# Batch 2 by transposed loads, early output tiles as 64x64 products, and a new order

## The chip, the cores and the metric

The kernel runs on one core of one Trainium2 chip. The metric is the device time of one execution in microseconds. The core has TensorE (PE; its weight loads are the row PEld), VectorE (DVE), ScalarE (ACT), GpSimd (POOL) and SyncE (SP), and 16 DMA engines, which all queues share. SP and POOL issue the DMAs of this kernel (ScalarE two at the start); each has a queue of its own.

## The reference

```python
# q, k, v: (8, 12, 448, 64); w_in (768, 2048), w_out (2048, 768)
scores = matmul(q, k.T) / sqrt(64)
m = max(scores)
e = exp(scores - m)
attn = e / (sum(e) + exp(-m) + 1e-09)
x = matmul(attn, v)            # heads side by side: (3584, 768)
h = x @ w_in
out = square(maximum(h, 0)) @ w_out
```

Attention for 8 batches of 12 heads, 448 tokens and head size 64, and then a two-layer block with a squared ReLU over all 3584 tokens.

## The kernel before

Everything is computed in fp16 with fp32 sums. A "quad" is four heads of a batch (three quads a batch). Scores are computed keys by queries, without the maximum: `e = exp(score)`, and the sum of `e` comes from an addition on VectorE and a product with ones. So a quad takes seven score steps (64 keys each), seven `exp` steps on ScalarE, four additions on VectorE, seven steps of values, and a reciprocal by Ln and Exp on ScalarE.

Scores need q and k with the 64 head dimensions on the partitions. There are two ways to get them.

- Batches in `ON_PE` (0, 1 and 2): POOL loads them in natural layout with a cast to fp16 (`load_natural_quads`, line 112), TensorE transposes them (`transpose_one`, line 194, 14 products for one of q or k of a quad), and VectorE or ScalarE copies them from PSUM into the tile `qk` (`transposed_copy`, line 201). A score step is then four 64x64 products of 448 columns.
- The others: POOL writes an fp16 copy of q and k of the batch to DRAM (`stage`, line 143), SP loads it transposed in three DMAs (`transposed_loads`, line 160: q, and k twice, shifted by a row), POOL copies the last keys apart (`tail_keys`, line 171), and V comes in four DMAs with another order of tokens. A score step is then eight 64x64 products of 224 columns.

The tile `qk` has two buffers, so batch 2's takes that of batch 0.

The whole is emitted in an order written out by hand (`ORDER`, line 662), whose steps are one letter with numbers (`STEPS`, line 624). It covers batch 0 (in halves of 224 queries), batches 1 and 2, and the first six output tiles. Its steps:

- `d` a load from the list `LOADS` (line 614), `c t u` the first quad's casts, transposes and copies, `T U` `transpose_one` and `transposed_copy` of (batch, quad, q or k)
- `s e` scores and exp. 0 to 23 are the halves of batch 0, 24 to 44 batch 1, 45 to 65 batch 2, seven steps a quad
- `p b y z n x` values, additions, sum, Ln, reciprocal and normalization of batch 0; `v a S Z M X` the same of a quad of the batches 1 and 2
- `i r g` a pair of first-layer blocks of batch 0, its ReLU and its square; `j k l` the same of one block of 128 of F of batch 1
- `o n,f0,f1` blocks f0 to f1 of the 16 blocks of F of output tile n (128 tokens by 384 columns; n even is the left half, n odd the right half), `O` its evacuation and store
- `P` closes the first PSUM pools and opens the ring of four banks, from which the tiles `mp` come

Each engine takes its instructions in this order, and so do the DMA queues of SP and POOL.

From batch 3 on five cycles follow (`CYCLE`, line 719), one a batch: the last quad of the batch before, scores and values of this one, output tiles `o`, `O`, `Q` and the first layer `j k l` of the batch before. Their output tiles are already computed as 64x64 products in two half sums (`out_piece` with `rows`, line 536): each block is four products, the upper 64 rows of F into one bank and the lower 64 into another. `O` (`out_first`) scales the first sum, `Q` (`out_second`) adds the other one, and only then is the tile stored. The six early tiles are single 128x128 products in one bank, with `out_done` (line 566).

In `store` (line 522) the tokens of a batch in `ON_PE` go out in pieces of 64 rows, of the others in pieces of up to 128.

Of the kernel before, what the change touches and what calls it, by code (L numbers as in the profile page):

```python
# [10 lines left out]
FP16 = mybir.dt.float16  # L11
# [5 lines left out]
def kernel(  # L17
# [9 lines left out]
    nc = tc.nc  # L27

    B, H, S, D = q.shape
# [4 lines left out]
    RUN = 4  # L34
    NQ = H // 4
    KC = S // 64
    ON_PE = (0, 1, 2)
    COLS = H * S // 2 + 16
    HALF = DM // 2
    FIRST = S // 2  # L40
# [55 lines left out]
    def load_v_quads(b, g0=0, g1=NQ):  # L96
        if b not in vns:
            vns[b] = v_pool.tile([128, 2, NQ, KC, D], FP16, name="vn")
        vn = vns[b]
        if b in ON_PE:  # L100
            if g1 - g0 == NQ:
                nc.gpsimd.dma_start(out=vn.rearrange("p j g c d -> p (j g) (c d)"), in_=by_pairs["v"][b])
            else:
                nc.gpsimd.dma_start(out=vn[:, :, g0].rearrange("p j c d -> p j (c d)"), in_=by_pairs["v"][b, :, g0::NQ])
            return
        for i in range(2):
            rows_ = vn[64 * i:64 * i + 64].rearrange("p j g c d -> p (j g) (c d)")
            for c0, c1 in ((0, KC - 1), (KC - 1, KC)):
                src = v[:, :, 64 * c0:64 * c1].rearrange("b (hp i) (p t) d -> b i p hp (t d)", i=2, t=c1 - c0)
                nc.gpsimd.dma_start(out=rows_[:, :, c0 * D:c1 * D], in_=src[b, i])  # L110
# [32 lines left out]
    def stage(b):  # L143
        for n, t in (("q", q), ("k", k)):
# [11 lines left out]
            if hi < lo + TOTAL:  # L156
                nc.gpsimd.dma_start(out=st[hi - lo:TOTAL].rearrange("(r w) -> r w", r=1),
                                    in_=src[0:lo + TOTAL - hi].rearrange("(r w) -> r w", r=1))

    def transposed_loads(b):  # L160
        qk = qks[b] = qk_pool.tile([128, 3, COLS], FP16, name="qk")
        for i, n, x, c in ((0, "q", FRONT, H * S // 2), (1, "k", FRONT, H * S // 2), (2, "k", 0, COLS)):
            nc.sync.dma_start(
                out=qk[:, i, 0:c],
                in_=stages[n, b][x:x + c * 2 * D].rearrange("(r c) -> r c", c=2 * D),
                transpose=True,
            )

    kms = {}

    def tail_keys(b):

        km = kms[b] = flat.tile([128, H, 64], FP16, name="flatq")
        for r in range(2):
            for odd in range(2):
                rows_ = slice(64 * r, 64 * r + 64)
                which, x = (1, 0) if odd == r else (2, odd)
                src = qks[b][rows_, which, x:x + H * S // 2].rearrange("p (h x) -> p h x", h=H)
                nc.gpsimd.tensor_copy(km[rows_].rearrange("p h (x o) -> p h x o", o=2)[:, :, :, odd],  # L179
                                      src[:, :, S // 2 - 32:S // 2])  # L180
# [418 lines left out]

    def load_quad(b, g):  # L600

        x = {(0, 1): (0, 0), (0, 2): (0, 1), (1, 0): (1, 0), (1, 1): (0, 0), (1, 2): (0, 1),
             (2, 0): (1, 0), (2, 1): (1, 1), (2, 2): (0, 0)}[b, g]
        if (b, x[0]) not in nats:
            nats[b, x[0]] = nat.tile([128, RUN * 2 * S], FP16, name=f"nn{x[0]}")
        load_natural_quads(b, (g,), x[1], nats[b, x[0]])

    def load_third():
# [2 lines left out]
        load_v_quads(3)  # L611
        stage(4)

    LOADS = ([lambda b=b, g=g: load_quad(b, g) for b in range(3) for g in range(NQ) if b + g]
             + [lambda b=b, g=g: load_v_quads(b, g, g + 1) for b in range(2) for g in range(NQ)]
             + [lambda: load_v_quads(2)]
             + [lambda i=i: load_win(i, NW) for i in range(NW)]
             + [lambda n0=n0, y=y: load_wout(n0, y, 2) for n0 in (0, HALF) for y in range(2)]
# [2 lines left out]
    def quad_visit(n):  # L621
# [29 lines left out]
        "v": lambda m, c: values_step(m, c),  # L651
        "X": lambda m: quad_x(m),
        "P": lambda n: other_ring(),
        "o": lambda n, f0, f1: out_piece(128 * (n // 2), HALF * (n % 2), HALF, range(f0, f1)),
        "O": lambda n, act: out_done(128 * (n // 2), HALF * (n % 2), HALF, act),
    }

    def other_ring():
# [1 line left out]
        ring.append(ctx.enter_context(tc.tile_pool(name="ring", bufs=4, space=bass.MemoryType.PSUM)))  # L660

    ORDER = """
        d0 W8 c1,4,0 c0,0,1 c1,0,1 t0,0,0 c0,4,1 t1,0,0 u0,0,0,0 t1,0,4 u1,0,0,0 t0,0,4 u1,0,4,0 s0 d8 d1 u0,0,4,0 t0,1,0 e0 t1,1,0 u0,1,0,0 u1,1,0,0 s1 s2 e1
        d10 t0,1,4 u0,1,4,0 t1,1,4 u1,1,4,1 T0,1,0 T0,1,1 s3 U0,1,0,0,4,0 e2 U0,1,1,0,4,0 s4 U0,1,0,4,7,1 e3 d9 U0,1,1,4,7,0 d2 p0 e4 p2 s16 p1 e16 b0,0 b0,1
        p3 b0,2 b0,3 s6 y0 d18 s5 T0,2,0 e6 U0,2,0,0,4,0 z0 T0,2,1 U0,2,1,0,4,0 e5 U0,2,1,4,7,0 U0,2,0,4,7,0 s7 s9 b1,0 n0 b1,1 e7 x0 s8 p4 e9 b1,2 d3 b1,3 p5
        e8 p6 p7 s10 y1 b2,0 p8 p9 e10 s11 p10 b2,1 z1 e11 b2,2 b2,3 s12 p11 s13 n1 x1 y2 e12 T1,0,0 U1,0,0,0,7,0 T1,0,1 z2 n2 s14 e13 x2 p12 p13 s15
        U1,0,1,0,7,0 e14 e15 s17 p14 b3,0 b3,1 e17 s18 i0,7 d17 d5 b3,2 e18 b3,3 p15 y3 z3 b4,0 r0,7,0 s21 s19 e21 T1,1,1 d4 n3 b4,1 i0,6 U1,1,1,0,7,0 s20 d15
        T1,1,0 x3 b4,2 e19 b4,3 d16 s23 p16 p17 p18 r0,6,0 U1,1,0,0,7,0 e20 b5,0 e23 s22 e22 b5,1 p19 y4 s26 z4 n4 i0,4 g0,7 x4 r0,4,0 s27 i0,5 g0,6 b5,2 e26
        s25 e27 T1,2,1 s28 e25 p20 p21 r0,5,0 p22 s24 g0,5 b5,3 e28 d11 T1,2,0 p23 e24 s29 y5 e29 U1,2,1,0,7,0 U1,2,0,0,7,0 T2,0,0 T2,0,1 U2,0,0,0,7,0 z5 g0,4
        d6 U2,0,1,0,7,0 s30 n5 s32 a0,0 e30 d13 i0,0 i0,1 s33 x5 e32 r0,0,0 g0,0 r0,1,0 s31 i1,0 d12 g0,1 e33 i0,3 r1,0,0 e31 r0,3,1 s35 d7 s36 e35 P0 e36  # L670
        i0,2 s34 e34 a0,1 a0,2 g1,0 v0,0 a0,3 S0 v0,1 v0,2 v0,3 v0,4 Z0 v0,5 v0,6 M0 r0,2,0 g0,3 g0,2 s37 i1,3 a1,0 a1,1 e37 X0 r1,3,0 a1,2 g1,3 i1,6 s39 s40
        a1,3 e39 i1,1 r1,1,0 r1,6,0 s43 T2,2,0 e40 d20 T2,2,1 g1,6 e43 s42 g1,1 e42 U2,2,0,0,7,0 s41 d19 i1,5 r1,5,0 e41 s38 e38 T2,1,0 T2,1,1 U2,2,1,0,7,0
        U2,1,0,0,7,1 S1 a2,0 Z1 s44 U2,1,1,0,7,0 i1,4 i1,2 a2,1 e44 r1,4,1 s45 a2,2 g1,5 a2,3 v1,0 v1,1 M1 v1,2 v1,3 v1,4 v1,5 v1,6 r1,2,1 v2,0 S2 v2,1 X1
        g1,4 e45 g1,2 v2,2 v2,3 v2,4 Z2 v2,5 v2,6 M2 s47 X2 s46 i1,7 j3,0,2 r1,7,0 o0,0,4 j3,2,4 j1,0,2 j3,4,6 k3,0 j12,0,2 o0,4,8 j1,2,4 o0,8,12 e46 e47
        o0,12,16 s50 d21 g1,7 s51 j12,2,4 j1,4,6 k1,0 j5,0,2 e51 e50 l3 j5,2,4 j5,4,6 d23 O0,1 k5,1 j12,4,6 l5 o1,0,4 s48 s49 j6,0,2 e49 l1 e48 d22 k12,1 l12
        o1,4,8 o1,8,12 o1,12,16 s53 s52 e52 e53 j6,2,4 j10,0,2 o5,0,4 j6,4,6 O1,1 s55 k6,0 s54 j10,2,4 o5,4,8 j0,0,2 e55 a3,0 j10,4,6 j8,0,2 o5,8,12 j0,2,4
        a3,1 k10,1 o5,12,16 e54 s61 s57 l6 a4,0 j14,0,2 O5,0 e57 j14,2,4 j14,4,6 e61 j8,2,4 a3,2 j9,0,2 j9,2,4 j0,4,6 j9,4,6 a3,3 j8,4,6 l10 s56 k0,0 k14,0
        e56 l0 k8,1 s58 o2,0,4 o2,4,8 l14 d14 s59 v4,0 v4,1 v4,2 v4,3 a4,1 v4,4 v4,5 e58 k9,0 s60 e59 s64 o2,8,12 d24 l9 o2,12,16 a4,2 a4,3 j7,0,2 e60 v4,6
        e64 S4 Z4 M4 O2,0 S3 j7,2,4 o4,0,4 l8 o4,4,8 o4,8,12 o4,12,16 j7,4,6 Z3 s62 X4 s63 M3 O4,0 v3,0 v3,1 v3,2 v3,3 v3,4 v3,5 e62 v3,6 s65 X3 k7,1 j4,0,2
        e65 o3,0,4 a5,0 o3,4,8 o3,8,12 o3,12,16 j15,0,2 j4,2,4 j4,4,6 l7 e63 j15,2,4 a5,1 j2,0,2 O3,1 a5,2 j2,2,4 a5,3 j15,4,6 k4,0 j13,0,2 j11,0,2 S5 Z5  # L680
        k15,0 M5 l4 l15 j2,4,6 k2,0 j13,2,4 l2 j11,2,4 j13,4,6 j11,4,6 k11,1 k13,1 l11 l13
    """

    for step in ORDER.split():
# [4 lines left out]
    def cycle(b):  # L689
        m = NQ * (b - 1) - 1  # L690
        first = EARLY + KC * (b - 3)

        def following():
            if b + 1 < B:
                transposed_loads(b + 1)
                tail_keys(b + 1)
                load_v_quads(b + 1)
                if b + 2 < B:
                    stage(b + 2)

        return {
# [20 lines left out]
        a1,1 o2,8,10 o2,10,12 o2,12,14 s2,3 o2,14,16 o3,0,2 s2,2 O2,0 o3,2,4 a1,2 Q2 o3,4,6 e2,3 e2,2 o3,6,8 s2,6 e2,6 o3,8,10 s2,0 e2,0 o3,10,12  # L722
        o3,12,14 o3,14,16 a1,3 s2,4 o5,0,2 e2,4 o5,2,4 o5,4,6 o5,6,8 s2,5 O3,0 s2,1 o5,8,10 o5,10,12 o5,12,14 o5,14,16 e2,5 e2,1 Q3 S1 v1,0 v1,1 Z1
        v1,2 v1,3 M1 v1,4 O5,0 v1,5 Q5 v1,6 X1 o6,0,2 s3,4 e3,4 o6,2,4 s3,0 e3,0 o6,4,6 o6,6,8 a2,0 o6,8,10 o6,10,12 s3,1 o4,0,2 o6,12,14 a2,1 s3,3
        e3,1 o4,2,4 o6,14,16 s3,2 e3,3 o4,4,6 O6,1 a2,2 o4,6,8 s3,5 a2,3 o4,8,10 Q6 o4,10,12 e3,2 e3,5 o4,12,14 o4,14,16 O4,1 Q4 a3,0 s3,6 v2,0 v2,1
        S2 Z2 v2,2 v2,3 v2,4 v2,5 M2 v2,6 e3,6 X2 j2,0,2 j2,2,4 j2,4,6 k2,0 j13,0,2 j13,2,4 l2 j13,4,6 j3,0,2 k13,1 l13 j3,2,4 j15,0,2 j12,0,2 j15,2,4
        j0,0,2 j3,4,6 a3,1 j15,4,6 k3,1 a3,2 k15,1 j12,2,4 a3,3 l15 j0,2,4 j0,4,6 l3 j12,4,6 j10,0,2 j10,2,4 j4,0,2 k0,0 l0 k12,1 l12 j10,4,6 j6,0,2
        j7,0,2 j7,2,4 j7,4,6 j4,2,4 k10,0 j6,2,4 j4,4,6 l10 j6,4,6 k7,1 j5,0,2 l7 j5,2,4 k4,1 j11,0,2 k6,0 j11,2,4 j11,4,6 j9,0,2 l6 j5,4,6 l4 j9,2,4
        j8,0,2 j8,2,4 k5,1 j9,4,6 l5 j1,0,2 k11,0 j8,4,6 j1,2,4 j1,4,6 k9,1 j14,0,2 j14,2,4 l11 l9 k8,0 j14,4,6 l8 k1,1 l1 k14,0 S3 Z3 d0 l14 M3
    """  # L730

    for b in range(3, B):
# [58 lines left out]
```

## Time and profile before

| | us |
|---|---|
| median of 3 runs (lowest, highest) | 396.51 (396.07, 397.43) |
| the profiled execution | 396.87 |
| its span, first to last instruction | 394.8 |
| one cycle (178.11 to 223.45, and on to 268.62, 313.79) | 45.2 to 45.3 |
| end of ORDER, start of the cycles | 105.9 |

The profiled execution's own time is 2.1 us over its span, and 0.1% over the median. TensorE's granted clock is 1.00 in all windows. Busy times are unions of what an engine's instructions cover; a matmul's own duration (0.32 us for 384 columns) has the length of the pipeline in it, so the price of a matmul is read from start to start.

Some groups of the page, in the form: line, engine, operation, tiles written and read, shapes, count, busy us and mean ns.

| group | count | mean ns |
|---|---|---|
| L208 DVE COPY, a transposed quad into `qk`, 128x896 | 11 | 619 |
| L206 ACT the same | 1 | 911 |
| L563 DVE the add of `Q`, 128x384 | 35 | 556 |
| L559 DVE the scaling of `O`, 128x384 | 23 | 556 |
| L557 ACT the scaling of `O`, 128x384 | 32 | 491 |
| L245 ACT exp of a score step, 128x896 | 122 | 917 |
| L179 POOL COPY, a part of `tail_keys` | 20 | 643 |

DMAs: a natural quad is two of 224 KB, a quad's V 224 KB, a piece of `win` 384 KB (eight of them), a piece of `wout` 768 KB (four), a staged q or k 676 KB. All of these KB count what is written.

### The profile page before, as it was taken

To read this page: it belongs to the slowest core of one execution; us is meant where nothing else is said; L and a number is where in the kernel's file an instruction comes from. 1 tells how busy PE (TensorE), PEld (TensorE's weight loads), DVE (VectorE), ACT (ScalarE), POOL (GpSimd) and SP (SyncE) were. 2 spreads that over 40 slices of the span, in tenths; PEclk is the share of its full clock that TensorE was granted. 3 is DMA by queue.
4 is the path that set the end of the run, shared out by engine and by line. 5 is a ranking of instruction groups with operands and counts; after the bars stand their busy time and mean duration, and the time that the engine had idled before them with its cause. 6 is when DMAs were issued, how large, how long until landed. Compare 5 with 4: busy or idle time off the path is not lost.

```text
span 394.8 us, 13877 instructions
## 1 busy us (share of the span) xinstructions
PE 385.5 (98%) x6252; PEld 262.9 (67%) x6252; DVE 240.5 (61%) x445; ACT 238.1 (60%) x324; POOL 59.8 (15%) x96
## 2 busy tenths in 40 slices
PE   8789999999999999999999999999999999999997
PEld 4567776445599766896579866776677765555665
DVE  3889994385746765668536876567646785285000
ACT  4999895768479625895279834896269934100111
POOL 8354500003200032000500016000500000000000
PEclk9999999999999999999999999999999999999999
DMA  8999999568942579419692398527652100100222
GB/s 146 203 204 206 203 206 208 98 127 154 191 85 63 113 140 181 96 43 161 113 203 75 77 193 127 129 64 141 126 74 68 58 7 2 62 0 14 68 80 81
DMA packets 75051, 45.33 MB, mean 115 GB/s; under 512 B 47472, under 2 KB 72944, under 8 KB 74992
## 3 DMA queue, kind: packets, MB, share of 16 engines
q0 software_dynamic: 24752, 22.62, 36.3%
q1 hardware_dynamic: 49952, 21.59, 25.0%
q8 instruction: 49, 0.80, 0.8%
q10 hardware_dynamic: 288, 0.23, 0.2%
q14 instruction: 10, 0.08, 0.1%
HBM read 45.69 MB, written 17.93 MB: 161 GB/s over the span
## 4 chain that ended last, share of the span: by engine, by line
PE 94%; DVE 3%; ACT 1%; issue 1%; DVEq 0%; ACTq 0%
PE mp L92 81%; PE sp L92 9%; PE xp L92 2%; PE mp L198 2%; ACT et L245 1%; DVE qk L208 1%; DVE half L334 1%; DVE half L332 0%; PE mp L225 0%; ACT rcp L356 0%; ACT rcp L363 0%; DVE qk L235 0%; DVE half L338 0%; DVE half L336 0%; DVE rt L496 0%
## 5 line engine op out<-in xcount | busy, mean ns | idle before, releaser
L92 PE MATMUL mp<-wout,gs 64*64 64x384 f16 (+2 forms) x2592 | 166.7, 322 | 0.0
L92 PE MATMUL mp<-xt,win 128*64 128x448 f16 (+2 forms) x1344 | 151.4, 339 | 0.1
L245 ACT ACTIVATE et<-sp 128x896 f16<-128x896 f32 (+1 forms) x131 | 110.8, 889 | 30.1 <-PE sp L92 28.9
L92 PEld LDWEIGHTS <-win 128*64 128x64 f16 (+1 forms) x1344 | 89.6, 106 | 58.7 <-issue 7.4
L92 PEld LDWEIGHTS <-gs 64*64 64x64 f16 (+1 forms) x2592 | 105.9, 106 | 34.3 <-issue 1.1
L494 ACT ACTIVATE rt<-mp 128x448 f16<-128x448 f32 x55 | 29.3, 544 | 57.2 <-PE mp L92 52.4
L500 DVE TENSOR_TENSOR gs<-rt 128x448 f16<-128x448 f16 x128 | 49.2, 401 | 22.2 <-ACT rt L494 19.8
L92 PE MATMUL sp<-qk 64*64 64x224 f16 (+1 forms) x1056 | 57.4, 274 | 2.5 <-issue 0.9
L496 DVE TENSOR_SCALAR rt<-mp 128x448 f16<-128x448 f32 x73 | 45.2, 621 | 23.0 <-PE mp L92 21.5
L557 ACT ACTIVATE ot<-mp 128x384 f32<-128x384 f32 (+2 forms) x34 | 16.4, 481 | 51.3 <-PE mp L92 50.8
L92 PEld LDWEIGHTS <-qk 64*64 64x64 f16 x1056 | 36.1, 114 | 14.4 <-issue 7.4
L179 POOL COPY flatq<-qk 64x384 f16<-64x384 f16 x20 | 12.4, 643 | 205.9 <-DMA qk<-stage_k 205.6
L245 ACT ACTIVATE nn<-sp 128x896 f16<-128x896 f32 x42 | 36.7, 915 | 1.9 <-PE sp L92 1.8
L478 DVE TENSOR_TENSOR xt<-mp,rcp 128x448 f16<-128x448 f32 x42 | 24.3, 620 | 20.0 <-ACT rcp L457 17.8
L92 PEld LDWEIGHTS <-vn 64*64 64x64 f16 x756 | 24.1, 107 | 9.8 <-issue 2.6
L563 DVE SCALAR_TENSOR_TENSOR ot<-mp,ot 128x384 f32<-128x384 f32 x35 | 19.5, 556 | 16.9 <-ACT ot L557 15.3
L454 ACT ACTIVATE rcp<-sp,one_b 128x896 f32<-128x896 f32 x21 | 21.2, 1007 | 10.0 <-PE sp L92 10.0
L92 PE MATMUL mp<-et,vn 64*64 64x448 f16 (+1 forms) x448 | 25.1, 343 | 0.0
L559 DVE TENSOR_SCALAR ot<-mp 128x384 f32<-128x384 f32 x23 | 12.8, 556 | 19.6 <-PE mp L92 19.5
L432 DVE TENSOR_TENSOR half<-et 128x1792 f16<-128x1792 f16 x15 | 16.3, 1087 | 7.0 <-ACT et L245 6.9
L457 ACT ACTIVATE rcp<-rcp 128x896 f32<-128x896 f32 x21 | 20.0, 952 | 0.6
L434 DVE TENSOR_TENSOR half<-half,et 128x1792 f16<-128x1792 f16 x15 | 16.4, 1091 | 0.7 <-ACT et L245 0.3
(59 smaller groups left out, 198.2 us busy)
## 6 DMA issues: line engine op xcount, KB each, us to landing
out_dram<-ot SPq DMA_DIRECT2D x52, 96.0 KB, 2.3
out_dram<-ot SPq DMA_DIRECT2D x19, 192.0 KB, 1.9
win<-in_moe_w_in_dram POOLq DMA_DIRECT2D x8, 384.0 KB, 11.1
wout<-in_moe_w_out_dram POOLq DMA_DIRECT2D x4, 768.0 KB, 15.6
vn<-in_v_dram POOLq DMA_DIRECT2D x10, 288.0 KB, 4.8
stage_q<-in_q_dram POOLq DMA_DIRECT2D x4, 676.0 KB, 8.8
stage_k<-in_k_dram POOLq DMA_DIRECT2D x4, 676.0 KB, 12.0
nn<-in_q_dram POOLq DMA_DIRECT2D x8, 224.0 KB, 8.1
```

Of the source, the lines that this page charges most:

```text
L92: return nc.tensor.matmul(out_, lhsT, rhs, start=start, stop=stop)
L245: nc.scalar.activation(out=out_, in_=in_, func=AF.Exp, scale=scale)
L432: nc.vector.tensor_add(esq[m], a[:, 0:w], a[:, w:2 * w])
L434: nc.vector.tensor_add(esq[m], esq[m], z[:, 0:w])
L454: nc.scalar.activation(out=rcp, in_=zp[:, :, 0:S], func=AF.Ln, bias=one_b)
L457: nc.scalar.activation(out=zqs[m], in_=zqs[m], func=AF.Exp, scale=-1.0)
L478: nc.vector.tensor_mul(xts[b][:, 2 * g + i, :], xqs[m][i][:, 0:S], zqs[m][:, i, :])
L494: nc.scalar.activation(out=rt[:, 0:m], in_=hp[:, 0:m], func=AF.Relu)
L496: nc.vector.tensor_scalar(out=rt[:, 0:m], in0=hp[:, 0:m], scalar1=0.0, scalar2=None, op0=ALU.max)
L500: nc.vector.tensor_mul(gs[:, f0:f0 + per, t0 % RING:t0 % RING + n], r, r)
L557: nc.scalar.activation(out=ot, in_=op[:, 0:w], func=AF.Copy, scale=OUT_SCALE)
L563: nc.vector.scalar_tensor_tensor(out=ot, in0=lo[:, 0:w], scalar=OUT_SCALE, in1=ot, op0=ALU.mult, op1=ALU.add)
```

## The change

1. `ON_PE` loses batch 2: its q and k are staged, loaded transposed, and its tail keys copied; `T2`, `U2` steps and three natural quads go. Its V comes in the four DMAs of the later batches, its scores are eight products of 224 columns, and its stores are in pieces of up to 128 rows.
2. The early tiles' `o` steps use `rows`, and `O` and `Q` replace `out_done`.
3. ORDER is another one. The loads of POOL now run `d0 d1 d8 d2 d10 d9 d3 d18 d15 d17 d16 d4 d5 d11 d19 d20 d12 d21 d13 d22 d7 d23 d14`, then `d24`, where `d5` is `stage(2)`, `d7` `tail_keys(2)`; `d6` is `transposed_loads(2)`, on SP. (Before: `d0 d8 d1 d10 d9 d2 d18 d3 d17 d5 d4 d15 d16 d11 d6 d13 d12 d7 d20 d19 d21 d23 d22 d14 d24`, where `d5`, `d6`, `d7` were natural quads of batch 2.)
4. In the cycles the one step `d0` becomes seven, with k loaded before q, and they stand before `a3,0` and no longer at the end.

```diff
-    ON_PE = (0, 1, 2)
+    ON_PE = (0, 1)
...
+    PLANES = (("k", FRONT, H * S // 2), ("k", 0, COLS), ("q", FRONT, H * S // 2))
+
+    def transposed_load(b, i):
+        qk = qk_of(b)
+        n, x, c = PLANES[i]
+        nc.sync.dma_start(
+            out=qk[:, (i + 1) % 3, 0:c],
+            in_=stages[n, b][x:x + c * 2 * D].rearrange("(r c) -> r c", c=2 * D),
+            transpose=True,
+        )
+
     def transposed_loads(b):
-        qk = qks[b] = qk_pool.tile([128, 3, COLS], FP16, name="qk")
-        for i, n, x, c in ((0, "q", FRONT, H * S // 2), (1, "k", FRONT, H * S // 2), (2, "k", 0, COLS)):
...
+        for i in range(3):
+            transposed_load(b, i)
...
-    LOADS = ([lambda b=b, g=g: load_quad(b, g) for b in range(3) for g in range(NQ) if b + g]
-             + [lambda b=b, g=g: load_v_quads(b, g, g + 1) for b in range(2) for g in range(NQ)]
+    LOADS = ([lambda b=b, g=g: load_quad(b, g) for b in ON_PE for g in range(NQ) if b + g]
+             + [lambda: stage(2), lambda: transposed_loads(2), lambda: tail_keys(2)]
+             + [lambda b=b, g=g: load_v_quads(b, g, g + 1) for b in ON_PE for g in range(NQ)]
...
-        "o": lambda n, f0, f1: out_piece(128 * (n // 2), HALF * (n % 2), HALF, range(f0, f1)),
-        "O": lambda n, act: out_done(128 * (n // 2), HALF * (n % 2), HALF, act),
+        "o": lambda n, f0, f1: out_piece(128 * (n // 2), HALF * (n % 2), HALF, range(f0, f1), True),
+        "O": lambda n, act: out_first(128 * (n // 2), HALF * (n % 2), HALF, act),
+        "Q": lambda n: out_second(128 * (n // 2), HALF * (n % 2), HALF),
...
+        c0,0,1 d0 c1,4,0 W8 c1,0,1 t0,0,0 u0,0,0,0 t1,0,0 c0,4,1 u1,0,0,0 t1,0,4 t0,0,4 u0,0,4,1 s0 d1 d8 u1,0,4,0 t0,1,0 u0,1,0,0 t1,1,0 s1 d2
...
+        g0,6 b5,0 p19 y4 b5,1 z4 n4 i0,0 i0,1 g0,7 s26 e27 x4 b5,2 p20 r0,0,0 r0,1,1 b5,3 s25 e26 e25 p21 p22 p23 y5 i0,5 g0,0 r0,5,0 s29 s24 z5 g0,1
+        n5 x5 g0,5 i0,4 i1,1 r0,4,0 e24 e29 r1,1,1 s28 d19 e28 s30 e30 P0 a0,0 i0,3 i1,4 a0,1 g1,1 g0,4 s33 s31 r1,4,0 r0,3,0 a0,2 g1,4 e33 i1,6
+        T1,2,0 T1,2,1 e31 U1,2,1,0,7,0 r1,6,0 s32 s34 d20 e32 i1,0 U1,2,0,0,7,1 g0,3 i0,2 e34 i1,5 s37 s35 g1,6 d12 r1,0,0 e37 i1,7 e35 r0,2,0 a0,3 S0
+        v0,0 v0,1 Z0 s40 v0,2 g1,0 r1,7,0 v0,3 v0,4 v0,5 v0,6 M0 s39 g0,2 e40 r1,5,0 a1,0 d21 d13 i1,2 s41 X0 e39 o0,0,4 e41 o0,4,8 s36 g1,7 r1,2,1
+        g1,2 s38 i1,3 e36 g1,5 s43 e38 o0,8,12 o0,12,16 e43 O0,1 a1,1 r1,3,0 s42 s44 g1,3 d22 o4,0,4 o4,4,8 e42 o4,8,12 a2,0 d6 a1,2 a1,3 Q0 s56
+        o4,12,16 e44 O4,1 S1 a2,1 Q4 a2,2 v1,0 v1,1 v1,2 a2,3 d7 v1,3 v1,4 Z1 e56 o2,0,4 o2,4,8 v1,5 S2 v1,6 M1 o2,8,12 o2,12,16 d23 X1 Z2 v2,0 v2,1
+        v2,2 v2,3 O2,1 Q2 v2,4 s53 o5,0,4 s45 v2,5 v2,6 M2 e53 s49 o5,4,8 e45 s60 X2 e49 o5,8,12 o5,12,16 s54 e60 s55 j8,0,2 O5,0 e54 j7,0,2 j7,2,4 Q5
...
-        def following():
+        def following(n):
             if b + 1 < B:
-                transposed_loads(b + 1)
-                tail_keys(b + 1)
-                load_v_quads(b + 1)
-                if b + 2 < B:
+                if n < 3:
+                    transposed_load(b + 1, n)
+                elif n < 5:
+                    tail_keys(b + 1, (n - 2,))
+                elif n == 5:
+                    load_v_quads(b + 1)
+                elif b + 2 < B:
                     stage(b + 2)
...
-        ... k1,1 l1 k14,0 S3 Z3 d0 l14 M3
+        ... O4,1 Q4 d0 d3 d6 d1 d4 d2 d5 a3,0 s3,6 ...
+        ... k1,1 l1 k14,0 S3 Z3 l14 M3
```

`tail_keys(b, planes)` copies, for each plane of k given, the two halves of partitions that come from it, instead of all four copies at once.

## The prediction

> **What bounds the kernel now.** I read the page's busy times first, then the chain that ended last.
>
> ```profile
> PE 385.5 (98%) x6252; PEld 262.9 (67%) x6252; DVE 240.5 (61%) x445; ACT 238.1 (60%) x324; POOL 59.8 (15%) x96
> PE 94%; DVE 3%; ACT 1%; issue 1%; DVEq 0%; ACTq 0%
> ```
>
> TensorE is both the busiest engine and 94% of the chain, so time is saved only by giving it fewer or shorter columns, and is lost wherever it is made to wait. The windows say where it idles: 4.7 us of 5 to 35 us, 0.1 us between there and 105.9 us, where the written order ends and the five cycles begin.
>
> The timeline of TensorE gives the prices. In 66 to 71 us, 12 products of 448 columns start 2.28 us before the next form (0.190 each), and 8 of 128x128x384 take 1.40 us to the start of the scores that follow: 8 x 0.162 plus 0.10. In 109 to 113 us the 64x64 form puts 32 products, eight blocks of F, into 1.30 us: 0.162 a block as well, and then the scores start with nothing added. So the 64x64 form is no faster by itself. What it avoids is the change between 128-row and 64-row products, some 0.09 to 0.10 us each. The transposes show such changes around them:
>
> ```profile
> 51.28 0.38 PE L92 MATMUL sp<-qk 64*64 64x448 f16 x4
> 51.59 0.97 PE L198 MATMUL mp<-ident,nn 128*64 128x128 f16 x28
> 52.49 0.57 PE L92 MATMUL sp<-qk 64*64 64x448 f16 x8
> 53.00 1.32 PE L92 MATMUL mp<-xt,win 128*128 128x224 f16 x12
> ```
>
> The pair of transposes runs 0.90 us until the next scores, and the scores before it lasted 0.31 us instead of 0.19: 1.02 us a pair.
>
> The DMA side decides the rest. By windows:
>
> ```profile
> 40.00:50.00 10.00, 9.87 (x128) 7.18 (x125) 9.69 (x18) 7.63 (x11) 5.58 (x7) 1.00 1.28 204
> 50.00:60.00 10.00, 10.00 (x168) 7.75 (x168) 9.20 (x17) 9.63 (x13) 0.00 (x0) 1.00 1.29 207
> 60.00:70.00 10.00, 10.00 (x100) 5.95 (x94) 4.83 (x10) 5.45 (x7) 0.00 (x0) 1.00 1.18 207
> ```
>
> The last two columns are the share of the 16 DMA engines and GB/s. From 10 to 70 us they are full with POOL's loads, at 203 to 207 GB/s. Nothing else runs on them then: the first output leaves at 70.8 us, the first transposed load at 83.6 us.
>
> **The change, part by part: TensorE.** The six `T2,...` steps go: three pairs at 1.02 us, 3.1 us, six changes of form among them. I counted the changes in both orders by their 64-row steps (`s p y S v`, now `o`) and 128-row steps (`t T i j`, formerly `o`): 64 before, 45 after. The other 13 at 0.093 us are 1.2 us. Batch 2's 21 score steps go from four products of 448 columns (0.189) to eight of 224 (0.192, from 110.56 to 110.76 us): +0.06 us. Sum: **-4.3 us**, all of it on the path, since TensorE has no other idle to fill.
>
> **Other engines.** VectorE loses five copies at 0.619 us and gains six `Q` adds at 0.556; ScalarE loses one copy at 0.911. Counting every step of the two orders by its row, VectorE has 81.9 us of work (83.4 before) and ScalarE 89.0 (88.0) in some 100 us: hidden behind TensorE. Without that cover the worst is ScalarE's 1 us. Early on it is ScalarE that paces TensorE: at step `P0` it has 37.4 us of work behind it against TensorE's 31.2 (40.5 against 35.2 before), so the idle of the first 40 us may move by up to 1 us either way; I take 0. Each early tile now holds two of the ring's four banks until `Q`. The cycles do the same without a wait, so 0, and at most six waits of one 0.556 add, 3.3 us.
>
> **The cycles.** `d0` to `d6` now stand in front of `a3,0` instead of at the end. On SP's queue nothing lies between the two places: the last store (`Q4`) is issued before, the next after the cycle's end. So the transposed loads start when they did. On POOL, `stage` now goes ahead of two copies and of the load of V, and shares the DMA engines with two transposed loads. Its 1352 KB took 6.5 us before (59.8 to 66.3), so loads that landed at 145 us land at most at 152, and the next cycle reads them from 178 us on. Covered by 26 us: 0. Larger stores for batch 2 and three more V issues of 0.66 us on POOL lie as far from any need: 0.
>
> **The order's loads.** The six natural loads of batch 2 (1344 KB) are replaced by `stage(2)` (1352 KB), equal work for POOL's queue. New are three transposed loads on SP. In the cycles, with the DMA engines to themselves, they look like this:
>
> ```profile
> 130.51 2.75 SPq L531 DMA_DIRECT2D out_dram<-ot  x4
> 133.36 3.22 SPq L163 DMA_TRANSPOSE qk<-stage_q  x1
> 136.68 6.34 SPq L163 DMA_TRANSPOSE qk<-stage_k  x2
> ```
>
> The last landed 5.75 us after its issue at 139.37: 11.8 us for the three, about 10.0 of it full use of the DMA engines. When can they start? They read what `stage(2)` writes. Ahead of its end on POOL's queue lie 7560 KB (first quad 224, quads 2240, V 672, `win` 3072, itself 1352). Before, 7552 KB had landed with the V load issued at 33.2 us, 11.6 us later: 44.7. I take 44.5 us. Behind it, up to the last `wout` (`d22`), are 3744 KB at 197 KB/us (the 768 KB of `wout` that landed from 52.0 to 55.9): 19.0 us.
>
> When are they needed? `s56`, the first scores of batch 2, needs all three. Ahead of it the new order has TensorE work of 52.1 us: warm-up 3.5, first transposes 3.3, ten `T` 3.8, scores 9.0, `p` and `y` 4.6, sixteen `i` 18.4, `v` and `S` 1.5, `o` 4.5, 37 changes 3.4. The same count gives 54.5 us at `o0` before, where the trace has 63.5: 9.0 of idle and of small gaps. So `s56` is reached at **61.1 us**, and `o0,8,12`, which needs the second `wout` (`d20`), at 57.5.
>
> Between 44.5 and 61.1 us lie 16.6 us, and the DMA engines have 10.0 us of transposed loads and 8.9 us of V and `wout` up to `d20` to move, with 10.1 us more queued behind. So something is late, unless SP's queue goes first and mixing raises the rate. How SP's queue fares beside POOL's is seen on stores:
>
> ```profile
> L531 SPq DMA_DIRECT2D out_dram<-ot x2: 466/718/969, 100.8 to 101.3; - x2
> DMA to landing us min/median/max: 6.6/7.1/7.5
> ```
>
> Alone, stores of the same size land in 2.1 to 2.2 us (114.6). Here POOL's loads were running. In the packet records no store packet moved before 104.5 us; then, to 107.5, 120 store packets stand beside 154 of POOL's: about one for one. A transposed load moves 256 B rows, 505 per DMA engine for the three, against 768 or 896 B for POOL's (304 per engine up to `d22`). One for one, POOL's queue ends first and the transposed loads end last: 44.5 + (19.0 + 10.0) = 73.5 us, or 71.6 with the 7% that the mixed store packets gained (267 and 78 ns, a pair in 0.32 us). From both sides: 56.3 if SP's queue goes first, 75.3 if it goes last with its full 11.8. I take 72.4, the store row being the nearest: **+11.3 us** of waiting at `s56`. Behind it in TensorE's queue stand all later steps, and nothing after 61 us has idle to give back.
>
> The Trainium skill (DMA: Bandwidth & Descriptors, Queues, rings and completion order) says that each DMA engine takes its queues in turn by packets of some 9 to 17 descriptors. With equal packets on both queues that gives the one for one above, by it the same sum. With long packets on SP's queue alone it gives rival 1.
>
> After such a pause TensorE may run slowly for a while. At launch its eight 512-column products took 3.5 us, 0.43 each, where 448 columns later take 0.19: half rate. That again costs 0 to 1.8 us; idles up to 0.9 us before show none, and a pause of 11 us is nearer the launch: I take 0.9. The Trainium skill (TensorE: Matmul & The Clock Gate, Part 1) puts the return to half rate after an idle window of about 3.4 us; by it the sum would have the 1.8. No run here shows it.
>
> **Sum**: -4.3 + 11.3 + 0.9 = +7.9. The profiled execution took 396.87 us (span 394.8), the median of the runs is 396.51; on the latter, **404.4 us**.
>
> **The rivals.**
> 1. *The transposed loads get most of the turns* (chance 0.19). They land near 58 to 61 us, but `d20` has then waited: 44.5 + 10.0 + 8.9 = 63.4 against 57.5 at worst, 62 at an even split by time. TensorE waits 4.5 to 5.9 us at `o0,8`: 396.7 to 398.1. For it: rows of 256 B are short, and sixteen in one turn would outweigh one of 768 B. Against: the store row.
> 2. *Hidden after all, faster* (0.22). The 18.9 us of both fit into the 16.6 with at most 2.5 us of waiting: 396.5 - 4.3 + 0 to 2.5 = 392.2 to 394.7. It needs a mixed rate 15% or more up, shared about evenly; for it, in 85 to 87.5 us transposed loads with a store moved 269 GB/s, while POOL's alone stay at 203 to 211. It turns to slower than before once the waiting passes 4.3 us.
> 3. *The transposed loads don't move until POOL's queue is dry* (0.09): 75.3, a wait of 14.2 and 1.8 of slow clock: 408.2. For it: nothing moved from 101 to 104.5 us; against: it did then.
>
> The forecast itself holds 0.50 (401 to 407). **Numbers**: a measurement here can tell 0.3% (1.2 us). Faster by more than that is rival 2, 0.22; within it are 0.08, most of rival 1's lower half; slower 0.70. The range from 393.0 to 407.0 us leaves out rival 3 and a part of rival 2; for the likeliest case alone 401 to 407.
>
> **What would show it.** TensorE: no `mp<-ident,nn` after 60 us, one run of early 64x64 `mp<-wout,gs` without 0.09 steps into scores. The wait: an idle of 8 to 12 us before `sp<-qk` near 61 us, ended by DMA `qk<-stage`; issue to landing of the first three transposed loads far above 6.5 us. Wrong if they land before 62 us, if TensorE waits at `mp<-wout,gs` instead (rival 1), or if DMA isn't full from 45 to 70 us.

## The result, and the profile after

The changed kernel takes **411.21 us** (median of 4 runs, 407.2 to 414.34) against 396.29 us for the kernel before beside it: a ratio of **1.0337, with an interval from 1.0257 to 1.0416**. One of the four runs (414.34) fell in a slower state of the chip; the ratio and all comparisons below use the other three (407.2, 410.56 and 411.85). The forecast was 404.4 us with a range from 393 to 407, so the direction was right and the time lies outside the range. The profiled execution took 411.85 us, with a span of 410.1 against 394.8: 15.3 us more.

The page after, busy times, the chain that ended last, and the clock in 40 slices:

```profile
PE 384.6 (94%) x6540; PEld 261.9 (64%) x6540; DVE 239.7 (58%) x443; ACT 238.6 (58%) x326; POOL 61.0 (15%) x99
...
PEclk9999995699999999999999999899999999999999
...
PE 77%; DMA 18%; SPq 2%; ACT 1%; POOL 1%; issue 0%; DVE 0%; ACTq 0%
```

TensorE is busy for as long as before (384.6 against 385.5 us) in a longer span, and DMA, which was not in the chain, now holds 18% of it. The clock drops in two places, between 61 and 82 us and near 260 us. The waits of TensorE and its timeline say what happened there (start, length, and in brackets the idle time ahead and what ended it):

```profile
PE sp L92 <- DMA qk<-stage_q: 17.6, 2, 14.9
```

```profile
56.23 1.49 PE L92 MATMUL mp<-wout,gs 64*64 64x384 f16 x32 [0.64 <-DMA wout<-in_moe_w_out_dram]
57.53 0.58 PE L92 MATMUL sp<-qk 64*64 64x448 f16 x8
57.91 2.15 PE L92 MATMUL mp<-wout,gs 64*64 64x384 f16 x48
74.96 0.59 PE L92 MATMUL sp<-qk 64*64 64x224 f16 x8 [14.90 <-DMA qk<-stage_q]
```

Two waits for transposed loads make 17.6 us. The first and large one is at `s56`, the first scores of batch 2: TensorE is done at 60.06 and resumes at 74.96. The run of 64x64 products ahead of it, broken only by scores, is what the change was to give. The second wait is in a cycle, at 258.00, and no part of the forecast had it.

The windows of 10 us (busy time of PE, PEld, DVE, ACT, POOL, then clock, share of the DMA engines, GB/s):

```profile
40.00:50.00 10.00, 10.00 (x143) 7.66 (x145) 7.30 (x16) 6.87 (x8) 0.88 (x1) 1.00 1.21 204
50.00:60.00 10.00, 9.36 (x178) 6.93 (x168) 8.53 (x15) 8.60 (x12) 0.00 (x0) 1.00 1.32 172
60.00:70.00 10.00, 0.06 (x4) 0.00 (x0) 0.55 (x1) 0.00 (x0) 1.21 (x2) 0.64 1.28 189
70.00:80.00 10.00, 5.04 (x64) 3.29 (x68) 1.71 (x3) 2.65 (x4) 4.88 (x8) 0.51 1.14 207
```

TensorE, VectorE and ScalarE all but stand still from 60 to 70 us, while the DMA engines are full and move less than before (189 GB/s against 207): the mixture of the two queues is slower than POOL's loads alone. The 172 GB/s of 50 to 60 us also hold about 1 us, from 57 to 58, in which both queues nearly stopped, at 8 to 54 GB/s by quarters of a microsecond. The three transposed loads, by the tile's view (issues on SP: length in ns, then when):

```profile
L165 SPq DMA_TRANSPOSE qk<-stage_k x2: 10247/11926/13606, 44.9 to 55.2; - x2
L165 SPq DMA_TRANSPOSE qk<-stage_q x1: 3878/3878/3878, 68.8 to 68.8; - x1
...
DMA to landing us min/median/max: 6.0/17.3/20.3
```

SP is held 10 and 14 us by the issue of the first two. They land at 65.2, 72.5 and 74.8. In the packet records the first transposed row moves at 48.8 us, 3.9 us after its issue, and from then the two queues take turns, row by row (the starts on either queue recur after 86 ns, which is 16 engines / 187 rows per us):

```
stretch (us)    POOL rows per us (768 B, some 896 B)    SP rows per us (256 B)
49 to 68        187 typically, mean 173                 187 typically, mean 174
57 to 58        24                                      26
71 to 74        none left                               999 to 1135
```

The stop near 57 us is in the packet records of experiments 1, 2, 6 and 8 as well, some have a second one near 64 us, and experiment 7 has its own at 54.5 and 64. The kernel before has none from 10 to 71 us, with POOL's queue alone. The cause of the stop stays open.

The difference of 15.3 us between the two spans divides at the first values of the first cycle (105.91 before, 118.31 after). The last term of each half is what remains when the others are taken out.

| up to there, +12.4 | us | behind it, +2.9 | us |
|---|---|---|---|
| wait at `s56` | +14.9 | wait at 258.00 | +2.7 |
| wait for `wout` at 56.23 | +0.6 | half clock behind it (72 products in 4.15 us instead of 2.8) | +1.4 |
| half clock behind `s56` (measured below) | +1.5 | the rest: the trace of before has a gap of 0.88 us in a cycle that is not there after | -1.2 |
| less idle in 5 to 35 us (3.45 against 4.66) | -1.2 | | |
| the rest: fewer and shorter products | -3.4 | | |

### The profile page after: what moved, and what is told of

The parts are those of the page before. It is cut to its first block, busy times and chain, and to the rows that moved or that the text cites. A ratio compares the mean times of both kernels' runs of the same rounds, so it can differ in the third digit from the quotient of the medians.

```text
span 410.1 us, 14467 instructions
## 1 busy us (share of the span) xinstructions
PE 384.6 (94%) x6540; PEld 261.9 (64%) x6540; DVE 239.7 (58%) x443; ACT 238.6 (58%) x326; POOL 61.0 (15%) x99
## 4 chain that ended last, share of the span: by engine, by line
PE 77%; DMA 18%; SPq 2%; ACT 1%; POOL 1%; issue 0%; DVE 0%; ACTq 0%
PE mp L92 68%; PE sp L92 8%; DMA wout<-in_moe_w_out_dram 7%; DMA qk<-stage_q 5%; DMA stage_q<-in_q_dram 4%; DMA win<-in_moe_w_in_dram 3%; SPq L165 1%; PE xp L92 1%; ACT et L253 1%; POOL nn L116 0%; POOL win L134 0%; PE mp L233 0%; PE mp L206 0%; ACT ot L565 0%; SPq L539 0%
## 5 line engine op out<-in xcount | busy, mean ns | idle before, releaser
L92 PE MATMUL mp<-wout,gs 64*64 64x384 f16 (+2 forms) x2880 | 168.8, 326 | 0.6 <-DMA wout<-in_moe_w_out_dram 0.6
L92 PE MATMUL mp<-xt,win 128*64 128x448 f16 (+2 forms) x1344 | 149.3, 339 | 0.1
L92 PEld LDWEIGHTS <-gs 64*64 64x64 f16 (+1 forms) x2880 | 104.0, 108 | 34.8 <-issue 1.6
L92 PE MATMUL sp<-qk 64*64 64x224 f16 (+1 forms) x1116 | 55.1, 267 | 19.7 <-DMA qk<-stage_q 17.6
L502 ACT ACTIVATE rt<-mp 128x448 f16<-128x448 f32 x55 | 29.2, 543 | 62.8 <-PE mp L92 54.9
L565 ACT ACTIVATE ot<-mp 128x384 f32<-128x384 f32 (+2 forms) x36 | 17.3, 481 | 68.6 <-PE mp L92 68.1
L92 PEld LDWEIGHTS <-qk 64*64 64x64 f16 x1116 | 35.1, 116 | 32.1 <-issue 24.1
L187 POOL COPY flatq<-qk 64x384 f16<-64x384 f16 x24 | 15.5, 647 | 213.8 <-DMA qk<-stage_k 175.3
L571 DVE SCALAR_TENSOR_TENSOR ot<-mp,ot 128x384 f32<-128x384 f32 x41 | 22.8, 555 | 34.4 <-ACT ot L565 28.8
L92 PE MATMUL mp<-et,vn 64*64 64x448 f16 (+1 forms) x448 | 26.6, 354 | 0.8 <-DVE half L344 0.8
L567 DVE TENSOR_SCALAR ot<-mp 128x384 f32<-128x384 f32 x21 | 11.7, 555 | 22.4 <-PE mp L92 22.3
```

Source lines behind the costliest of these rows:

```text
L92: return nc.tensor.matmul(out_, lhsT, rhs, start=start, stop=stop)
L502: nc.scalar.activation(out=rt[:, 0:m], in_=hp[:, 0:m], func=AF.Relu)
L565: nc.scalar.activation(out=ot, in_=op[:, 0:w], func=AF.Copy, scale=OUT_SCALE)
L571: nc.vector.scalar_tensor_tensor(out=ot, in0=lo[:, 0:w], scalar=OUT_SCALE, in1=ot, op0=ALU.mult, op1=ALU.add)
```

## The experiments

"After" in a label's text is the changed kernel. Theory A is the reading above: TensorE loses what the transposed loads arrive late, and these are late because they share the DMA engines with POOL's loads row by row. The order strings are shown cut. Times are medians, beside runs of the kernel before of 396.1 to 396.9 us.

**1. The staging back at the end of a cycle's loads.**

```diff
-        ... O4,1 Q4 d0 d3 d6 d1 d4 d2 d5 a3,0 ...
+        ... O4,1 Q4 d0 d3 d1 d4 d2 d5 d6 a3,0 ...
```

> The changed kernel, with the staging of the batch after next as the last of the six steps in the cycles and no longer third; nothing else. Theory A (staging, issued on POOL right after the first two tail copies, shares the DMA engines descriptor by descriptor with the third transposed load, which then lands after the next cycle wants it): the 2.7 us wait before the scores at 258 us in the profile goes, the third transposed loads of the cycles land in 5 to 7 us instead of 7 to 16, the time is 407 to 409 us and the runs lie closer together than the 7 us of the changed kernel. Rival B (the place of the steps in the cycle, ahead of a3, causes the wait): no change, 411 us and a wait of 2 to 3 us in a cycle. Both: the wait of about 15 us at the first scores of batch 2 stays.

407.56 us (407.07 to 407.86), ratio 1.0292 [1.0273, 1.031]. That is 3.0 us below after's 410.56, but one of after's runs took 407.2 and the two intervals overlap, so the time alone does not show a gain. The traces show the cause. In the cycle that had the wait, the third transposed load of after and then of this kernel:

```profile
L165 SPq DMA_TRANSPOSE qk<-stage_q x1: 3456/3456/3456, 241.7 to 241.7; - x1
...
DMA to landing us min/median/max: 5.2/5.6/16.3
```

```profile
L165 SPq DMA_TRANSPOSE qk<-stage_q x1: 3180/3180/3180, 241.5 to 241.5; - x1
...
DMA to landing us min/median/max: 5.2/5.4/5.9
```

The third load, `q`, takes 5.2 us instead of 16.3, and no cycle waits. So `d6` in third place, right behind the issue of the last transposed load, is the cause of the second wait: the staging's loads on POOL's queue then run beside it. In after's packet records the two queues move 50 to 60 rows each per us from 246 to 249 us, again one for one. The staging's rows have 3584 B here (this is the last batch's; in the cycle that starts near 163 us they have 3328 B, and the third load landed 2 us before its use). After's run of 407.2 has the same mean clock as experiment 1's profiled run (0.983, against 0.975 in after's profiled one), so the wait may not come in every execution; that run has no trace. The wait at `s56` stays (14.95 us).

**2. The seven steps at the end of the cycle, in the order of after.** This tells the place from the order.

```diff
-        ... Q4 d0 d3 d6 d1 d4 d2 d5 a3,0 ... S3 Z3 l14 M3
+        ... Q4 a3,0 ... S3 Z3 d0 d3 d6 d1 d4 d2 d5 l14 M3
```

> The changed kernel with the seven load steps of a cycle back at its end, in the new order among themselves (staging third). Theory A (the order on POOL's queue counts, not the place, since SP and POOL have nothing else between the two places): as the changed kernel, 408 to 413 us, with third transposed loads that take over 7 us and at times a wait at a cycle's first scores. Rival B (the place counts): 407 to 409 us, no such wait.

415.08 us (410.48 to 415.81), ratio 1.0455 [1.0396, 1.0513], not below after, and above the 408 to 413 expected. The profiled execution, 410.48, still has the wait, and its third load again takes 16.1 us:

```profile
257.93 0.40 PE L92 MATMUL sp<-qk 64*64 64x224 f16 x8 [2.53 <-DMA qk<-stage_q]
```

The order makes the wait, not the place. Why the other three runs took 415 is not in a trace; their mean clock was 0.971 to 0.975, against 0.983 in the profiled one.

**3. The early tiles alone.** The kernel before, with `o`, `O` and `Q` of after and each `Q` right behind its `O`; nothing else of the change.

```diff
-        ... d23 O0,1 k5,1 ... O1,1 s55 ... O5,0 e57 ...
+        ... d23 O0,1 Q0 k5,1 ... O1,1 Q1 s55 ... O5,0 Q5 e57 ...
```

> The kernel before, with the six early output tiles alone as 64x64 products in two half sums (each Q right after its O). Theory A (the form is no faster, only the changes between 64-row and 128-row products cost, 0.093 us each): the order before then has 76 changes instead of 64, so 1.1 us slower: 397.0 to 398.0 us (ratio 1.002 to 1.004). Rival B (two banks of the ring of four for a tile make TensorE wait for the second evacuation): waits at mp<-wout,gs of 0.5 us and more each, up to 3.3 us: 398 to 400. Rival C (the form is faster by itself): below 396.

406.42 us (405.92 to 406.91), ratio 1.026 [1.0243, 1.0278]: above what any of the three gave. TensorE, which idled 0.1 us there, now waits 7.2 us for banks of the ring to be emptied:

```profile
66.49 0.54 PE L92 MATMUL mp<-xt,win 128*128 128x448 f16 x2 [0.72 <-DVE rt L496]
...
79.64 0.32 PE L92 MATMUL mp<-wout,gs 64*64 64x384 f16 x1 [1.35 <-ACT ot L557]
```

Rival B's mechanism holds, at more than its price. The order ends at 116.45 instead of 105.91 us; the waits are 7.2 of these 10.5, twelve more changes of form 1.1 by the price of 0.093, and some 2 us stay unexplained. In after's own order, where other work stands between the tiles and their `Q`, no such wait is in the trace: there the two banks are free because the order was rewritten for them.

**4. POOL's later loads held back.** Experiment 1, with the transposed loads and the tail keys in front of `d21`. POOL's copy of the tail keys waits for the loads of k, and what stands behind it in POOL's queue is issued only then.

```diff
-        ... a1,0 d21 d13 i1,2 ... a2,0 d6 a1,2 ... a2,3 d7 v1,3 ...
+        ... a1,0 d6 d7 d21 d13 i1,2 ... a2,0 a1,2 ... a2,3 v1,3 ...
```

> As e1_stage_last, and in addition the tail keys of batch 2 (which wait for its transposed loads) stand ahead of the last V, wout and V loads (d21, d13, d22) on POOL's queue, so that POOL issues those only after the transposed loads have landed. Theory A (POOL's queue and the transposed loads take turns descriptor by descriptor, and the transposed loads end only when POOL's queue runs dry): POOL then has 1984 KB and not 3744 KB left beside them, 10 us of loads, so they land at about 45 + 10 + 10 + 2 = 67 us, the wait at the first scores of batch 2 is 6 to 8 us instead of 15, and the time 399 to 402 us. Rival B (the transposed loads are slow whatever stands behind, some 30 us): landing at 75 us, 407 to 409 us.

399.63 us (398.68 to 400.06), ratio 1.0086 [1.0066, 1.0106], 7.9 us less than experiment 1. The three loads have landed by 65.3:

```profile
65.45 0.59 PE L92 MATMUL sp<-qk 64*64 64x224 f16 x8 [5.25 <-DMA qk<-stage_q]
...
77.58 1.49 PE L92 MATMUL mp<-wout,gs 64*64 64x384 f16 x32 [0.53 <-DMA wout<-in_moe_w_out_dram]
```

Theory A holds, with a wait a little under the 6 to 8 us it gave: no byte less is moved, only other bytes first, and the wait falls from 14.95 to 5.25 us while the late `wout` costs 0.5.

**5. The scores later as well.** Experiment 4 with `d13` ahead and the second half of the order rewritten: values of batch 1 and tile 2 come before `s56`, the other scores of batch 2 lie between first-layer blocks, and tiles 5, 1 and 3 follow later.

```diff
-        ... a1,0 d6 d7 d21 d13 i1,2 ... Q0 s56 o4,12,16 ... v1,4 Z1 e56 o2,0,4 ... v2,6 M2 e53 s49 o5,4,8 ...
+        ... a1,0 d13 d6 d7 d21 i1,2 ... Q0 o4,12,16 ... v1,4 Z1 o2,0,4 ... v2,6 X2 d23 d14 s56 s53 e56 e53 j8,0,2 ...
```

> As e4_hold_wout with the order of the second half of ORDER rewritten (same steps): d13 ahead of the tail keys on POOL's queue, and on TensorE the first scores of batch 2 come after the values of batch 1 and tile 2, some 6 us later; the first layer of batch 1 goes ahead of the right half tiles 5, 1, 3, whose wout lands last. Theory A (the wait for the transposed loads is the whole loss, and nothing else in the change costs): no wait over 2 us at the first scores of batch 2, TensorE without other waits, and 392 to 395 us, ratio 0.990 to 0.996, faster than the kernel before. Rival B (the loss only moves: wout or V are late instead, or ScalarE is behind with 21 exps in fewer us): 396 to 400 us with waits at mp<-wout,gs or sp<-qk that name a DMA or ACT et.

394.66 us (10 runs, 393.86 to 396.4), ratio **0.9966 [0.995, 0.9983]**: 0.3% below the kernel before. The wait is almost gone, and the clock stays at 1.00:

```profile
64.94 1.65 PE L92 MATMUL mp<-et,vn 64*64 64x448 f16 x28
66.97 0.59 PE L92 MATMUL sp<-qk 64*64 64x224 f16 x16 [0.38 <-DMA qk<-stage_q]
...
92.97 0.40 PE L92 MATMUL sp<-qk 64*64 64x224 f16 x8 [0.92 <-ACT rcp L462]
```

The rewritten order has new small waits of its own (0.3 to 0.9 us at six places, 3.3 us together), so it gains less than the products save.

**6 and 8. The wait filled.** Experiment 1 with 60, then 86, products of constants ahead of `s56`, whose results nobody uses. They take nothing off the wait; they were to show what the slow clock costs.

```diff
-        ... a1,3 Q0 s56 ...
+        ... a1,3 Q0 f60 s56 ...
```

(`f86` in experiment 8.)

> As e1_stage_last, with 60 products of constants (448 columns, 0.19 us each, some 11.3 us, results not used) ahead of the first scores of batch 2, so that TensorE is busy for most of its wait. Theory A (the pause also halves TensorE's clock from about 63 to 79 us, which costs 1.9 us after the wait): granted clock 1.00 until the rest of the wait, below 4 us, is over; 405 to 406.5 us, 1 to 2 us less than e1_stage_last at 407.6. Rival B (the clock costs nothing here): 407.6 us or a little more.

408.63 us (407.64 to 409.17), ratio 1.0317 [1.0297, 1.0337]: the expectation missed. 60 products leave an idle of 4.07 us, and the clock falls all the same. Hence 86:

> As e6_keep_busy with 86 products of constants in place of 60, so that TensorE is busy (16.3 us, from about 59.9 to 76.2 us) until the transposed loads have landed (75.6 us in e6_keep_busy). Theory A (a pause of over about 4 us halves the clock, which costs 1.7 to 1.9 us after it): granted clock 1.00 throughout, no idle before the first scores of batch 2, and with them at 76.2 us instead of 74.7 in e1_stage_last, but at the full clock at once: 407 to 407.6 us, that is the same time as e1_stage_last for a start of the scores 1.5 us later, and under e6_keep_busy (408.6, scores at 75.7, clock 0.5). Rival B (the clock costs nothing): 409 us.

407.94 us (407.48 to 410.52), ratio 1.0304 [1.027, 1.0337]. The same stretch in experiments 1, 6 and 8 (PE, clock, DMA share, GB/s):

```profile
75.00:77.50 2.50, 2.50 (x40) 0.50 1.03 142
```

```profile
75.00:77.50 2.50, 1.81 (x28) 0.52 1.05 143
```

```profile
75.00:77.50 2.50, 2.50 (x37) 1.00 1.05 153
```

From the first scores of batch 2 to the first values of the cycles, experiment 8 takes 41.58 us and experiment 1 43.07: the slow clock costs **1.5 us**, by one trace of each. In the time of the whole kernel it is not seen, and the median is no lower: the loads landed 1.3 us later in this execution (75.82), and the 86 products ran on to 76.6, so the scores started at 76.59 instead of 74.67.

**7. The staging two loads earlier.** Experiment 1, with `d5` (the staging of batch 2) in front of `d16`.

```diff
-        ... p14 p15 d16 b4,0 y3 d4 s23 ... e21 d5 p16 ...
+        ... p14 p15 d5 d16 b4,0 y3 d4 s23 ... e21 p16 ...
```

> As e1_stage_last, with the staging of batch 2 (d5) two loads further ahead on POOL's queue, before the second piece of win and the last natural quad: it lands at about 37 us instead of 45, and the transposed loads are issued 8 us sooner. Theory A (row by row in turn with POOL's queue, the transposed loads have the same share of a fixed amount of DMA work, and end when all that is queued is moved): they still land at 73 to 76 us, the wait at the first scores stays near 15 us or goes in part to a wait for wout, 406.5 to 409 us. Rival B (three transposed loads take 30 us beside other loads, whenever they start): landing at 67 us, wait 7 us, 399 to 401 us.

409.87 us (409.18 to 410.95), ratio 1.0354 [1.0333, 1.0375], just above the 406.5 to 409 expected.

```profile
42.97 4.12 PE L92 MATMUL mp<-xt,win 128*128 128x224 f16 x24 [4.86 <-issue]
...
77.02 0.59 PE L92 MATMUL sp<-qk 64*64 64x224 f16 x8 [10.97 <-DMA qk<-stage_q]
```

The first transposed load is issued 5 us sooner (39.77) and the last one lands no sooner (76.88): with all of POOL's loads still to share with, an earlier start only makes the mixed stretch longer. The products with `win`, whose last piece now lands at 42.88 instead of 36.21, wait too. Rival B, a landing at 67 us, falls.

**9 and 11. Experiment 5 with less waiting.** Sums and normalization of batch 2 moved away from the places where experiment 5 waited.

```diff
-        ... Q5 S4 o1,8,12 o1,12,16 a3,0 Z4 O1,1 ... v4,5 v4,6 X4 S3 Z3 s62 s59 ...
+        ... Q5 o1,8,12 o1,12,16 a3,0 O1,1 ... v4,5 v4,6 S4 Z4 Q3 j6,0,2 j6,2,4 j6,4,6 S3 M4 Z3 M3 ...
```

> As e5_late_scores, with the end of ORDER rearranged once more: the sums of the two quads (S4, S3) and their Ln and Exp stand where no exp of scores is queued ahead of them on ScalarE, and the additions of the last quad stand earlier on VectorE. Theory A (what keeps e5_late_scores from the full 4.3 us are its own waits of 3.3 us after 35 us and six more changes of form): the waits at sp<-half,ones and sp<-qk after 80 us (0.8, 0.9, 0.5 us) go, 392.5 to 394 us. Rival B (other queues are behind by then, the waits only move): 394 to 396 us.

394.1 us, ratio **0.9934 [0.9915, 0.9953]**, just above theory A's range and at the low end of rival B's. Experiment 11 is the same kernel, run again for its profile:

> The kernel of e9_late_scores_2 unchanged, for a profile beside e10_whole_tiles on the same chip: 393.5 to 394.5 us, TensorE's waits after 35 us together below 2.5 us (3.5 in e5_late_scores).

394.62 us (10 runs, 393.69 to 396.84), ratio **0.9945 [0.9923, 0.9967]**. From 35 us to the cycles TensorE has three waits, 2.6 us in all against 3.3 in experiment 5. Time and waits are just over what was expected (394.5 and 2.5). No other version has a lower ratio than experiment 9, but the intervals of experiments 5, 10 and 11 overlap with its own.

**10. The same without the 64x64 tiles.** Experiment 9, with the six early tiles as single 128x128 products again and without `Q`: 74 changes of form instead of 54.

```diff
-        "o": lambda n, f0, f1: out_piece(128 * (n // 2), HALF * (n % 2), HALF, range(f0, f1), True),
-        "O": lambda n, act: out_first(128 * (n // 2), HALF * (n % 2), HALF, act),
-        "Q": lambda n: out_second(128 * (n // 2), HALF * (n % 2), HALF),
+        "o": lambda n, f0, f1: out_piece(128 * (n // 2), HALF * (n % 2), HALF, range(f0, f1)),
+        "O": lambda n, act: out_done(128 * (n // 2), HALF * (n % 2), HALF, act),
+        "Q": lambda n: None,
```

> As e9_late_scores_2 (394.1 us), with the six early tiles as single 128x128 products in one bank again (no Q). Theory A (the 64x64 form saves only the changes of form, which are 74 in this order without it and 54 with it, at 0.093 us): 1.9 us slower, 395.5 to 396.5 us. Rival B (the two banks of a tile cost waits in this order too, as in e3_tiles_only, so that one bank gives them back): no change or faster, 392.5 to 394.3 us.

394.56 us (11 runs, 393.43 to 397.41), ratio 0.9941 [0.9916, 0.9965], the same time as experiment 11 in the same comparison, and between the two expectations. TensorE's waits between 35 us and the cycles, here and in experiment 11 (us, times, longest):

```profile
PE mp L92 <- DMA wout<-in_moe_w_out_dram: 0.6, 1, 0.6
PE sp L92 <- DVE half L446: 0.6, 1, 0.6
```

```profile
PE mp L92 <- issue: 1.2, 1, 1.2
PE sp L92 <- DVE half L446: 0.9, 1, 0.9
PE sp L92 <- DMA qk<-stage_q: 0.5, 1, 0.5
```

The whole tiles have 1.4 us less of waiting beside twenty changes more (1.9 us by the price of 0.093). The timelines show that two small effects cancel. From the first product of an early tile to the first values of the cycles, here and in experiment 11:

```profile
54.46 1.48 PE L92 MATMUL mp<-wout,gs 128*128 128x384 f16 x8
...
106.77 1.52 PE L92 MATMUL mp<-nn,vn 64*64 64x448 f16 x28
```

```profile
52.59 1.48 PE L92 MATMUL mp<-wout,gs 64*64 64x384 f16 x32
...
104.92 1.52 PE L92 MATMUL mp<-nn,vn 64*64 64x448 f16 x28
```

Both stretches take 52.3 us. Here 51.05 of it are work and 1.26 idle, in experiment 11 49.63 and 2.70. So the 64x64 form saves 1.4 us of work, 0.07 us for each of the twenty changes, and this order gives it back in waits. In the time, the second part of the change is worth nothing measurable here.

## Why the prediction was right or wrong

**What bounds the kernel** was read rightly. Nothing that TensorE loses after 61 us is given back: as its waits go, first in the cycle and then at `s56`, experiments 1, 4 and 5 take 407.6, 399.6 and 394.7 us.

**TensorE, -4.3.** -3.4 by the account. The same count for experiments 5 and 11 (six and nine changes of form more than after) gives 3.7 and 3.4, and their traces leave 2.7 and 2.5. So all three are 0.9 to 1.0 us short. A part is the price of a change of form: at 0.07 us (experiments 10 and 11) the 13 changes give 0.9 instead of 1.2. The rest stays open; the ends of products are modelled in a trace, so some of it can be idle that is misread.

**The wait at `s56`, +11.3: the mechanism held, the size was off.** It measured 14.9. TensorE got there at 60.06 instead of 61.1; the first 35 us idled 1.2 us less, a little over the "1 us either way" that I had set at 0. That makes the wait longer and costs nothing. The loads landed at 74.83 instead of 72.4, and these 2.4 us cost. One row for one row was right to the row; wrong was that mixing may gain 7%. A pair of rows took 16 / 187 = 86 ns of each engine, where 768 B alone take 61 ns (0.20 MB/us) and 256 B alone 15: mixing costs 12%. I had read the gain off 3 us of store packets, and took the middle between gain and none; nothing in that row was a transposed load. The stop from 57 to 58 us, some 1 us, was not in the sum. Neither were the 3.9 us until a first row moves, but POOL's rows moved at their full rate meanwhile (254 to 263 per us).

The Trainium skill (DMA: Bandwidth & Descriptors, Queues, rings and completion order) has the engines take their queues in turn by packets of some 9 to 17 descriptors. The trace agrees on the turns but not on their length: it shows one row on each side. By bytes this gave the transposed loads a quarter, 0.048 against 0.144 MB/us. Rival 1 needed long turns for SP's queue and is refuted.

**The clock, +0.9.** Experiment 8 measured 1.5, near the upper bound of 1.8. The clock fell at 62.8, after the end of work at 60.06, and in the cycle after an idle of only 2.1 us. The Trainium skill (TensorE: Matmul & The Clock Gate, Part 1) speaks of an idle window of about 3.4 us, free-running. The traces agree on the window, whose grid of 3.41 us is shown in the last section, but the one in the cycle was not idle throughout.

**The cycles, 0: this is the step that failed.** "Its 1352 KB took 6.5 us before ..., so loads that landed at 145 us land at most at 152, and the next cycle reads them from 178 us on. Covered by 26 us." Both halves were wrong. The next cycle does not begin to read at 178: its first scores follow the end of the cycle, at 152.47 us for the loads that landed at 145.12, so the cover was 7.4 us. That would still have hidden the 6.5. But the staging did not only add its own 6.5 us: the third load took 16.3 instead of some 5 us, 11 more, since its rows alternate with the staging's, as at 49 to 68 us, and beside rows of 3584 B only 50 to 60 of them move per us. The wait of 2.7 us with the slow clock behind it makes 4.1 us in the span, and the same stretch of experiment 1's trace is 4.2 us shorter. It is the largest single term that the sum missed. I had used the price of the staging alone on a queue, in the same text in which I worked out what a shared queue does to transposed loads.

**Other engines and the two banks, 0.** They held in the order of after. "At most 3.3" for the banks was too low as a bound: in experiment 3 TensorE waited 7.2 us. I had counted a `Q`'s own length, not that the ring then stalls every later tile.

**The rivals.** Rival 2 (hidden, 392.2 to 394.7) needed the mixture to be 15% faster, and it was slower; experiments 5, 9, 10 and 11 reach its time by moving the bytes and the scores, which the change did not. Rival 3 named the size of the wait (14.2 us) with the wrong mechanism: rows of SP's queue moved from 48.8 us on, long before POOL's last row at 70.5.

**The range** ended at 407.0. Without the failed step the time is 407.56 (experiment 1), still 0.56 us outside: the wait at `s56` and the clock both came out at the far end of their bounds, and the products saved 0.9 us less.

## What to carry to other kernels

A transfer with short rows that is started beside a queue full of long ones gets its share by rows, not by bytes: what helps is to hold the other queue's later loads back, or to move the first use, while an earlier start alone helped nothing here. When a load is moved, look up where its first use stands in the timeline (and what else is on the engines until then), and price it at the shared rate. A tile that holds two banks of a ring until a second step needs an order written for it.

## What the runs showed of the hardware

- Two queues that both have work alternated one for one: 187 rows of 256 B beside 187 rows of 768 B in a typical microsecond of 19, and 50 to 60 of each where the other rows had 3584 B. Alone, the short rows ran at 999 to 1135 per us.
- The issue of a transposed load held SP for 10.2 and 13.6 us under that load, and 2.3 to 4.6 us in the cycles of before.
- The clock changes on a grid of 3.41 us, in the clock records of all traces. Its stretches at half clock are whole numbers of that: 17.06 and 3.41 us in after, 13.65 in experiments 1 and 2, 6.83 in experiment 4, 3.41 in experiment 6. So an idle shorter than a window can be enough, and its place on the grid counts. In after, the window that ended at 257.39 us had TensorE at work for its first 1.3 us; the clock fell, and came back at 260.80, after a window with 2.8 us of work. In experiment 2 an idle of 2.53 us at the same place fell across two windows with 2.0 and 2.3 us of work each, and the clock stayed at 1.00. How much work a window needs does not come out of these runs. Around 258 us, for after (PE, PEld, DVE, ACT, POOL, clock, DMA share, GB/s):

```profile
257.25:257.50 0.25, 0.00 (x0) 0.00 (x0) 0.00 (x0) 0.00 (x0) 0.00 (x0) 0.77 1.35 126
257.50:257.75 0.25, 0.00 (x0) 0.00 (x0) 0.00 (x0) 0.00 (x0) 0.00 (x0) 0.50 1.30 203
...
260.75:261.00 0.25, 0.25 (x12) 0.19 (x7) 0.00 (x0) 0.00 (x0) 0.00 (x0) 0.90 0.00 0
```

With work from 258.00 on, the clock was back after 2.8 us; behind the long wait at `s56` it took 4.9 us, from 74.96 to 79.9, since the first window there, to 76.48, had only 1.5 us of work.
